# Retention attention and a snake-activated layer on one core: a new order and new engines for all steps, a wait ahead of batch 2's loads, and two banks for the last two sums

## The chip, the core and the metric

The kernel runs on one core of a Trainium2 chip. The metric is the device time of one execution in microseconds. An engine here is one of TensorE (PE in the profile; PEld are its weight loads), VectorE (DVE), ScalarE (ACT), GpSimd (POOL) and SyncE (SP), which only issues transfers.

## What is computed

```python
# q, k, v: (8 batches, 8 heads, 576 positions, 64); gamma[h] = 1 - 2**(-5-h)
scores = q @ k.T / 8
ret    = scores * where(i >= j, gamma[h] ** (i - j), 0)
x      = (ret @ v), heads side by side        # (4608 tokens, 512)
h      = x @ w_in                             # (4608, 2048)
s      = sin(alpha * h)
g      = h + s * s / (alpha + 1e-9)
out    = g @ w_out                            # (4608, 512)
```

## The kernel before, in words

The 4608 tokens are cut into nine blocks of 512: blocks 0 to 7 are positions 0 to 511 of batches 0 to 7, and block 8 gathers the last 64 positions of all eight batches. The decay gamma**(i-j) is folded into q and k when they are cast to fp16, and the attention goes over in chunks of 128 positions with a running state between chunks.

One text, `STEPS`, holds every step of the program in the order in which it is issued. A step is a name, its numbers, and an engine after a colon where there is a choice (V is VectorE, A ScalarE, G GpSimd, P TensorE). Each engine takes its own steps in that order, and waits with semaphores for what they need. A word such as `raw.2.k.1=14` gives a buffer or a PSUM bank its place, so the text also sets when a buffer or a bank is used again. The loop at the end of the function (lines 934 to 954) reads the text; there a word `<NAME` adds a wait for an earlier step.

The steps that the change and the prediction speak of are these, with n the block and u one of the 16 units of 128 columns of `w_in`:

- `LD.b.k.p` (line 432) loads half p of k, q or v of batch b, 512 KB, on SP's queue. `WI.g` and `WO.g` (lines 402, 405) load the quarters of `w_in` and `w_out` on GpSimd's queue and cast them to fp16.
- `CA` (line 455; for v line 332) casts and scales what was loaded. `XP` (line 487) turns k and q with a transposing transfer on SP's queue; batches 0 and 1 are turned on TensorE instead (`TU`, line 473, copied out by `TK`).
- `SC` (line 558) makes scores, `MK` (line 571, VectorE) masks them, `VA` and `VB` (line 589) multiply them with v, `SA` (line 625) adds the state's share, `KP` copies the result out. `OU` (line 506) makes the chunks' state; `EV`, `TS`, `MA`, `MB`, `NS` and `ST` (lines 332 to 545) carry it on.
- `PR.n.u` (line 776) makes one unit of `x @ w_in` in a bank with four products of 512 columns (or two halves of 256). `SI` (line 784, ScalarE) takes the sine, `SQ` squares it (line 794 on ScalarE, 795 on VectorE or GpSimd), `PD` (line 799, VectorE) makes g and so sets the bank free.
- `G2.0.c` (line 815) makes block 0's output. Blocks 1 to 8 use a scheme of seven products for a two by two block matrix (`PP.n.p`, line 882, four groups j each), with sums of parts of g made beforehand by `SM` (line 863) and of `w_out` by `TT` (line 851).
- `CP` copies a product's bank out, `AD` (line 900) adds a bank to it, and `OQ` (lines 906 and 907) writes a quarter of the block to memory with two transfers. For the very last quarter `AD.8.12` and `OQ.8.12` are cut into two halves of 256 columns; the second transfer of each half goes out from ScalarE's queue, the rest from SP's.
- `KB` (line 419) are products with zeros that fill TensorE's waits at the start.

For block 8 the order within product 3 is by halves of the columns: `PP.8.3.0` and `PP.8.3.1` make columns 0 to 255, `PP.8.3.2` and `PP.8.3.3` columns 256 to 511, all in bank Z.

Of the kernel before, what the change touches and what calls it, by code (L numbers as in the profile page):

```python
# [960 lines left out]
```

## Time and profile before

| | |
|---|---|
| median of 3 runs | 302.37 us (302.0 to 302.52) |
| the profiled execution | 303.11 us, span 301.2 us |
| TensorE busy | 288.2 us (96%) |
| VectorE busy | 248.0 us (82%) |
| GpSimd busy | 190.9 us (63%) |
| ScalarE busy | 189.0 us (63%) |
| transfers | 49.88 MB, mean 166 GB/s |

The span is the time from the first to the last instruction; the profiled execution's own time is 1.91 us longer. Busy time is an average over stages that differ: in the first 60 us the weights and the first batches arrive, and the rest is products nearly without a break. TensorE's granted clock stands at 9 or more tenths in all 40 slices. Instructions of one line that follow each other are put together in the timeline, with "x8" for their number, and the time in brackets is how long the engine sat idle before the first of them, and for whom.

### The profile page before, as it was taken

Reading aid. Unit: us, or ns where it says so; the run is one execution under the profiler, and the core shown is the slowest. Engines: PE = TensorE matmul, PEld = TensorE weight load, DVE = VectorE, ACT = ScalarE, POOL = GpSimd, SP = SyncE. Lnnn points to the kernel's source line nnn. Section 1 sums busy time; section 2 is a strip of 40 time slices with the busy share of each in tenths; the row PEclk is TensorE's granted clock in tenths of the full one; section 3 lists DMA queues with packets and bytes.
Section 4 is the critical chain, followed back from the end, with each engine's and each line's share of the span. In section 5 each row is a group of like instructions: output and inputs, shape, how many; then the busy total and the mean of one; then the engine's idle time right before and its main releaser. Section 6 shows DMA issues by size and latency. Waiting matters only on the chain.

```text
span 301.2 us, 8721 instructions
## 1 busy us (share of the span) xinstructions
PE 288.2 (96%) x3625; PEld 185.6 (62%) x3625; DVE 248.0 (82%) x362; ACT 189.0 (63%) x302; POOL 190.9 (63%) x171
## 2 busy tenths in 40 slices
PE   7999999898999999999999999999999999999994
PEld 4665445453666656666675667666666576456883
DVE  2577899988998899998699999899887957579941
ACT  1645952769765895976737765783655366877420
POOL 6747863479858746957698529865755524894320
PEclk9999999999999999999999999999999999999999
DMA  7999999999979699669889773346457072004154
GB/s 226 316 253 232 216 221 316 326 199 257 214 194 249 171 228 180 166 161 152 196 182 195 177 168 98 88 93 143 106 131 134 0 191 55 2 2 104 37 125 119
DMA packets 119510, 49.88 MB, mean 166 GB/s; under 512 B 69792, under 2 KB 118960, under 8 KB 119472
## 3 DMA queue, kind: packets, MB, share of 16 engines
q1 hardware_dynamic: 114880, 44.97, 63.7%
q0 software_dynamic: 4224, 4.19, 8.2%
q8 instruction: 28, 0.46, 0.7%
q10 hardware_dynamic: 368, 0.18, 0.2%
q14 instruction: 10, 0.08, 0.1%
HBM read 36.74 MB, written 9.44 MB: 153 GB/s over the span
## 4 chain that ended last, share of the span: by engine, by line
PE 47%; DVE 5%; ACT 2%; issue 1%; DVEq 0%; ACTq 0%
PE banks L882 23%; PE banks L776 21%; DVE g L799 2%; ACT s L784 1%; ACT s L794 1%; PE banks L558 1%; PE banks L589 1%; DVE r L863 1%; PE banks L506 0%; DVE h L571 0%; DVE h L332 0%; DVE h L455 0%; DVE h L900 0%; DVE h L531 0%; PE banks L625 0%
## 5 line engine op out<-in xcount | busy, mean ns | idle before, releaser
L776 PE MATMUL banks<-r,w_in 128*128 128x512 f16 (+1 forms) x608 | 139.0, 368 | 1.9 <-DVE g L799 1.3
L784 ACT ACTIVATE s<-banks,alpha 128x512 f16<-128x512 f32 x144 | 95.4, 688 | 41.8 <-PE banks L776 39.0
L799 DVE SCALAR_TENSOR_TENSOR g<-s,inva,banks 128x512 f16<-128x512 f16 x144 | 102.4, 741 | 18.8 <-ACT s L794 13.5
L776 PEld LDWEIGHTS <-w_in 128*128 128x128 f16 x608 | 57.4, 98 | 54.7 <-issue 4.1
L882 PEld LDWEIGHTS <-g 128*128 128x128 f16 x640 | 61.4, 98 | 17.1 <-POOL g L863 0.4
L795 POOL TENSOR_TENSOR s<-s 128x512 f16<-128x512 f16 x36 | 38.0, 1060 | 40.0 <-ACT s L784 32.4
L882 PE MATMUL banks<-w_out,g 128*128 128x256 f16 x384 | 50.2, 273 | 0.3 <-DVE g L799 0.3
L332 ACT COPY h<-banks 128x512 f32<-128x512 f32 (+2 forms) x37 | 23.8, 643 | 36.6 <-PE banks L882 25.6
L794 ACT ACTIVATE s<-s 128x512 f16<-128x512 f16 x73 | 44.6, 629 | 2.0 <-PE banks L589 0.7
L455 POOL TENSOR_TENSOR h<-r,cn 128x1024 f16<-128x1024 f32 (+1 forms) x23 | 36.7, 1600 | 12.7 <-DMA r<-in_q_dram 11.8
L863 POOL TENSOR_TENSOR r<-g 128x1024 f16<-128x1024 f16 x15 | 31.9, 2131 | 11.9 <-DVE g L863 7.3
L571 DVE TENSOR_TENSOR h<-banks,mask 128x1024 f16<-128x1024 f32 (+1 forms) x32 | 35.4, 1116 | 4.0 <-PE banks L558 3.9
L882 PE MATMUL banks<-r,g 128*128 128x256 f16 x256 | 34.7, 273 | 0.0
L882 PEld LDWEIGHTS <-r 128*128 128x128 f16 x256 | 25.0, 98 | 6.3
L332 ACT CAST r<-banks 128x1024 f16<-128x1024 f32 (+1 forms) x18 | 16.1, 892 | 14.1 <-PE banks L589 8.0
L900 DVE TENSOR_TENSOR h<-banks,h 128x512 f32<-128x512 f32 (+1 forms) x25 | 16.5, 665 | 8.3 <-PE banks L882 5.6
L795 DVE TENSOR_TENSOR s<-s 128x512 f16<-128x512 f16 x35 | 19.8, 571 | 3.1 <-ACT s L784 3.0
L455 DVE TENSOR_TENSOR h<-r,cn 128x1024 f16<-128x1024 f32 (+1 forms) x17 | 18.4, 1088 | 4.8 <-DMA r<-in_k_dram 4.0
L863 POOL TENSOR_TENSOR g<-g,r 128x1024 f16<-128x1024 f16 x6 | 14.2, 2370 | 7.4 <-DVE r L863 7.4
L534 POOL TENSOR_TENSOR r<-h,r 128x256 f32<-128x256 f32 x12 | 9.4, 784 | 12.5 <-DVE h L531 10.1
L545 POOL TENSOR_TENSOR h<-r,cn 128x256 f16<-128x256 f32 x19 | 14.2, 751 | 3.7 <-DVE r L534 2.1
L882 PE MATMUL banks<-r 128*128 128x256 f16 x128 | 16.3, 273 | 0.0
(67 smaller groups left out, 274.5 us busy)
## 6 DMA issues: line engine op xcount, KB each, us to landing
out_dram<-h SPq DMA_DIRECT2D x70, 128.0 KB, 2.4
r<-in_q_dram SPq DMA_DIRECT2D x16, 512.0 KB, 5.5
r<-in_k_dram SPq DMA_DIRECT2D x10, 512.0 KB, 6.0
r<-in_v_dram SPq DMA_DIRECT2D x10, 512.0 KB, 11.2
r<-in_k_dram SPq DMA_DIRECT2D x24, 128.0 KB, 4.0
r<-in_v_dram SPq DMA_DIRECT2D x24, 128.0 KB, 4.2
w_in<-in_moe_w_in_dram POOLq DMA_DIRECT2D x4, 512.0 KB, 10.0
w_out<-in_moe_w_out_dram POOLq DMA_DIRECT2D x4, 512.0 KB, 13.9
```

The lines of the kernel that those rows point to most:

```text
L332: return eng.copy(d_, s_) if eng is nc.scalar else eng.tensor_copy(d_, s_)
L455: return eng.tensor_tensor(dst[:, a0:a1].rearrange("p a r t d -> p t (a r) d"), t_.rearrange("p (t a) x -> p t a x", t=2)[:, :, a0:a1].rea ...
L545: return eng.tensor_tensor(state_of(b, c), sum_of(b, c), decays(), MULT)
L571: return nc.vector.tensor_tensor(ret(b, p, y).rearrange("p t (z x) -> p (t z) x", z=2)[:, :, 0:n], bank(f"sc.{b}.{p}.{y}", 2).rearrange("p ...
L776: i = matmul(bank(hps)[:, cols], w_in16[:, a, u * P : (u + 1) * P], x_of(n)[:, a, cols], start=starts(hps), stop=(a == KT - 1), skip_group ...
L784: return nc.scalar.activation(small(f"s.{name}")[:, cols], bank(f"hps.{name}")[:, cols], mybir.ActivationFunctionType.Sin, bias=0.0, scale ...
L794: return nc.scalar.activation(ss_t, s_t, mybir.ActivationFunctionType.Square)
L795: return eng.tensor_tensor(ss_t, s_t, s_t, MULT)
L799: return nc.vector.scalar_tensor_tensor(g_of(n)[:, u, cols], small(f"ss.{name}")[:, cols], inva[:, u : u + 1], bank(f"hps.{name}")[:, cols ...
L863: return eng.tensor_tensor(S[s], a, b, op)
L882: i = matmul(ps[:, 256 * c : 256 * c + 256], left[:, 0, 128 * c : 128 * c + 128], right[:, 0, :], start=starts(f"{BANK_OF[p]}.{n}"), stop= ...
L900: return nc.vector.tensor_tensor(x, bank(f"{b}.{n}")[:, cols], x, ADD)
```

## The change

Four things change. The text `STEPS` is written in another order throughout, and many steps have another engine: 30 go from GpSimd to VectorE, 33 from VectorE to GpSimd, 23 each way between VectorE and ScalarE, 17 from GpSimd to ScalarE and 11 the other way (markers of the kind `RL` counted in). `LD.2.k.1`, the first load of batch 2, gets a wait for `WO.1`, and the nine loads after it come in a new order. For block 8, products 5 and 3 write their columns 0 to 255 to bank Z and 256 to 511 to bank Y. And the sum `AD.8.22` is cut into halves as `AD.8.12` was.

```diff
-TS.1.0:A; LD.2.q.0 raw.2.q.0=0; SI.0.12 s.0.12=15; SC.1.0.1 sc.1.0.1=0; PD.0.15; TU.1.k.1.2 tr.1.k.1=2
+TS.1.0:A kvs.1=15; PR.0.13.2 hps.0.13=4; TS.1.1:A; LD.2.k.1 raw.2.k.1=14 <WO.1; MA.1.1:G s32.1.1=27; PD.0.15
...
-PP.8.4.0; PP.8.3.2; CP.8.4:A c21.8=10; PP.8.3.0; OQ.8.21; PP.8.3.1; PP.8.3.3; AD.8.12.0; AD.8.12.1; OQ.8.12.0
-OQ.8.12.1
+PP.8.4.0; OQ.8.22; PP.8.4.2; PP.8.3.1; CP.8.4:A c21.8=10; PP.8.3.0; OQ.8.21; PP.8.3.3; AD.8.12.0; PP.8.3.2; AD.8.12.1
+OQ.8.12.0; OQ.8.12.1
...
     def PP(n, p, j):
-        ps = bank(f"{BANK_OF[p]}.{n}")
+
+        rows = ("Z", "Y") if n == 8 and p in (5, 3) else (BANK_OF[p],) * 2
...
                 i = matmul(
-                    ps[:, 256 * c : 256 * c + 256], left[:, 0, 128 * c : 128 * c + 128], right[:, 0, :],
-                    start=starts(f"{BANK_OF[p]}.{n}"), stop=True, skip_group_check=True,
+                    bank(f"{rows[c]}.{n}")[:, 256 * c : 256 * c + 256],
+                    left[:, 0, 128 * c : 128 * c + 128], right[:, 0, :],
+                    start=starts(f"{rows[c]}.{n}.{p in (5, 3)}"), stop=True, skip_group_check=True,
                 )
...
         cols = slice(0, 512) if h == 2 else slice(256 * h, 256 * h + 256)
+        if h == 1:
+            b = "Y"
```

The first place is SP's queue, where batch 2's loads begin. Before, `LD.1.v.1` and the next eight loads (`r` is the buffer of the loads; DMAHW are the lanes of SP's transfers):

```order
L432 DMA r_67<-in_v_dram 128x8x128 [waits DMAHW6_49]
L432 DMA r_67<-in_k_dram 128x8x128 [waits DMAHW7_49]
L432 DMA r_67<-in_q_dram 128x8x128 [waits DMAHW0_49,DVE_49,Pool_49]
L432 DMA r_67<-in_k_dram 128x8x128 [waits DMAHW1_49,DVE_49]
L432 DMA r_67<-in_v_dram 128x8x128 [waits DMAHW2_49,Activation_49]
L432 DMA r_67<-in_q_dram 128x8x128 [waits DMAHW3_49,DVE_49]
L432 DMA r_67<-in_v_dram 128x8x128 [waits DMAHW4_49,Activation_49]
L432 DMA r_67<-in_q_dram 128x8x128 [waits DMAHW5_49,DVE_49]
```

The same place now (line numbers are one less):

```order
L431 DMA r_67<-in_v_dram 128x8x128 [waits DMAHW6_49]
L431 DMA r_67<-in_k_dram 128x8x128 [waits DMAHW7_49,DMASW5_49]
L431 DMA r_67<-in_q_dram 128x8x128 [waits DMAHW0_49,DVE_49,Pool_49]
L431 DMA r_67<-in_q_dram 128x8x128 [waits DMAHW1_49,DVE_49]
L431 DMA r_67<-in_v_dram 128x8x128 [waits DMAHW2_49,Activation_49]
L431 DMA r_67<-in_k_dram 128x8x128 [waits DMAHW3_49]
L431 DMA r_67<-in_q_dram 128x8x128 [waits DMAHW4_49,DVE_49]
L431 DMA r_67<-in_v_dram 128x8x128 [waits DMAHW5_49]
```

The second row of the new piece is `LD.2.k.1`; DMASW5 is the lane of the second quarter of `w_out` on GpSimd's queue. Batch 2's v.0 moved from the fourth to the seventh of these loads, and batch 2's q.1 and v.1 moved ahead of it.

The second place is VectorE where block 1's first units are finished (the rows of line 799 are `PD.1.13`, `PD.1.6` and so on, line 851 is `TT`, line 795 is `SQ`). Before:

```order
L851 TENSOR_TENSOR r_67<-w_out_65,r_67 128x1024
L455 TENSOR_TENSOR h_68<-r_67,cn 128x2x8x64
L851 TENSOR_TENSOR r_67<-w_out_65,r_67 128x1024
L795 TENSOR_TENSOR s_69<-s_69 128x512
L799 SCALAR_TENSOR_TENSOR g_70<-s_69,inva,banks 128x512 x2
L795 TENSOR_TENSOR s_69<-s_69 128x512
L851 TENSOR_TENSOR r_67<-w_out_65,r_67 128x1024
L799 SCALAR_TENSOR_TENSOR g_70<-s_69,inva,banks 128x512 x3
```

Now:

```order
L850 TENSOR_TENSOR r_67<-w_out_65,r_67 128x1024
L454 TENSOR_TENSOR h_68<-r_67,cn 128x2x8x64
L850 TENSOR_TENSOR r_67<-w_out_65,r_67 128x1024
L798 SCALAR_TENSOR_TENSOR g_70<-s_69,inva,banks 128x512 x2
L794 TENSOR_TENSOR s_69<-s_69 128x512
L850 TENSOR_TENSOR r_67<-w_out_65,r_67 128x1024
L454 TENSOR_TENSOR h_68<-r_67,cn 128x2x8x64
L798 SCALAR_TENSOR_TENSOR g_70<-s_69,inva,banks 128x512 x3
```

The first square, `SQ.1.13`, left VectorE for GpSimd, and a cast of batch 3, `CA.3.q.1`, came to VectorE behind the first two `PD` of block 1.

The third place is the end of VectorE's program, from the sum `AD.8.11` on (line 900 is `AD`, line 332 the copy `CP.7.4`). Before:

```order
L900 TENSOR_TENSOR h_68<-banks,h_68 128x512 x2
L863 TENSOR_TENSOR g_70<-g_70,r_67 128x4x256
L332 COPY h_68<-banks 128x512
L900 TENSOR_TENSOR h_68<-banks,h_68 128x512
L900 TENSOR_TENSOR h_68<-banks,h_68 128x256 x2
```

Now:

```order
L903 TENSOR_TENSOR h_68<-banks,h_68 128x512
L862 TENSOR_TENSOR r_67<-g_70 128x1024
L862 TENSOR_TENSOR g_70<-g_70,r_67 128x4x256
L903 TENSOR_TENSOR h_68<-banks,h_68 128x512
L903 TENSOR_TENSOR h_68<-banks,h_68 128x256 x4
```

The copy went to ScalarE, and the last sums are four halves instead of one whole and two halves.

More of the change, by code (lines that the diff above doesn't have):

```diff
@@ new lines @@
+PR.0.12.2 hps.0.12=6; CA.1.v.0.2:V v16.1.0=22; SQ.0.6:A ss.0.6=4; PR.0.15.1; PD.0.3; SI.0.7 s.0.7=5
+PR.0.14.2 hps.0.14=2; SQ.0.5:V ss.0.5=2; SI.0.12 s.0.12=3; SQ.0.7:V ss.0.7=6; PR.0.10.2 hps.0.10=4; PD.0.7
+SI.0.14 s.0.14=1; SQ.0.9:A ss.0.9=7; PD.0.5; G2.0.3.0 op.0.3=7; SQ.0.14:G ss.0.14=8; SI.0.10 s.0.10=10; PD.0.6
+TU.1.k.0.2 tr.1.k.0=0; SQ.0.10:A ss.0.10=11; PD.0.14; G2.0.1.0 op.0.1=5; SI.0.15 s.0.15=9; PD.0.9
+CA.1.k.1.2:G k16.1.1=23; TK.1.k.0.2:A kT.1.0=24; PD.0.10; OU.1.0 kv.1.0.0=1 kv.1.0.1=2; SQ.0.15:V ss.0.15=12
@@ new lines @@
+CA.2.q.1.2:V q16.2.1=14; PR.1.6.2 hps.1.6=7; LD.3.q.0 raw.3.q.0=11; PR.1.13.1; TT.2.1:V; SI.1.6 s.1.6=14
+PR.1.9.2 hps.1.9=3; CA.2.k.0.2:V k16.2.0=6; SI.1.13 s.1.13=2; PR.1.4.1; FI.0.1:A osb.0.1=7; LD.3.k.0 raw.3.k.0=9
+SQ.1.13:G ss.1.13=6; G2.0.2.3 op.0.2=2; TT.4.1:V T4=12; SQ.1.6:A ss.1.6=5; SI.1.5 s.1.5=1; PR.1.7.2 hps.1.7=5
+CA.2.k.1.0:G; CA.2.v.1.2:A v16.2.1=15; LD.4.k.0 raw.4.k.0=10; PD.1.13 gT.1=1; G2.0.0.2; PD.1.6
+CA.2.v.0.2:A v16.2.0=12; PR.1.3.2 hps.1.3=4; SQ.1.5:V ss.1.5=10; SI.1.7 s.1.7=4; TT.4.0:V; G2.0.2.1
@@ new lines @@
+XP.2.q.1 qT.2.1=23; PR.1.0.0 hps.1.0=3; SI.1.1 s.1.1=1; MB.2.2:G; SC.2.0.1 sc.2.0.1=6; SI.1.10 s.1.10=2; PD.1.8
+PR.1.11.2 hps.1.11=4; FI.0.2:A osb.0.2=22; CA.3.q.0.2:G q16.3.0=21; MK.2.0.1 ret.2.0.1=2; PR.1.2.2 hps.1.2=1
+SI.1.11 s.1.11=14; SI.1.2 s.1.2=4; SC.2.0.0 sc.2.0.0=6; LD.3.v.1 raw.3.v.1=0; PR.1.0.1; ST.2.1:G s16.2=4
+MK.2.0.0 ret.2.0.0=26; SQ.1.2:A ss.1.2=10; XP.3.q.1 qT.3.1=25; ST.2.0:G; SQ.1.10:A ss.1.10=6; CA.3.k.0.1:G
+SI.1.0 s.1.0=7; VA.2.0 o.2.0=6; PD.1.10; SQ.1.11:A ss.1.11=5; RL.2.0:P; SA.2.0; VB.2.0; TT.3.0:V
@@ new lines @@
+PP.4.4.3; PD.5.5; PP.4.3.2; SQ.5.8:A ss.5.8=6; XP.7.k.1 kT.7.1=16; ST.6.2:G; PR.5.9.2 hps.5.9=2; CP.4.4:A c21.4=26
+PD.5.8; RL.6.1:G; MA.6.3:G s32.6.3=19; SQ.5.10:A ss.5.10=11; PP.4.3.1; SM.5.3.1:G; SI.5.9 s.5.9=12
+PR.5.14.2 hps.5.14=1; AD.4.12; SQ.5.9:A ss.5.9=4; PD.5.10; SA.6.1; VA.6.0 o.6.0=6; VB.6.1; PD.5.9
+OU.7.2 kv.7.0=0 kv.7.1=3; RL.6.0:G; MB.6.3:G; KP.6.1.2:A x.6=11; CA.7.q.1.2:V q16.7.1=3; VB.6.0; SA.6.0
+PP.5.1.1 X.5=2; SI.5.14 s.5.14=14; PR.5.12.2 hps.5.12=4; KP.6.0.2:A; SM.5.1.0:V; XP.7.q.1 qT.7.1=15
@@ L230 @@
+CP.8.2:A p2.8=11; PP.7.3.2; AD.8.11; PP.7.3.1; PP.7.4.0; SM.8.2.1:V; PP.8.6.0; SM.8.4.0:V; SM.8.4.1:G; PP.8.6.3
+PP.8.6.1; AD.7.12; PP.8.6.2; OQ.7.12; PP.8.5.3 Z.8=3; CP.8.6:A u2.8=6; PP.8.5.1; CP.7.4:A c21.7=18; PP.8.7.0; OQ.7.21
+PP.8.7.1; PP.8.7.3; PP.8.7.2; PP.8.5.0; OQ.8.11; CP.8.7:A u3.8=22; PP.8.5.2; PP.8.4.1; AD.8.22.0; PP.8.4.3; AD.8.22.1
+PP.8.4.0; OQ.8.22; PP.8.4.2; PP.8.3.1; CP.8.4:A c21.8=10; PP.8.3.0; OQ.8.21; PP.8.3.3; AD.8.12.0; PP.8.3.2; AD.8.12.1
+OQ.8.12.0; OQ.8.12.1
 """
```

382 lines of the change are left out of this document (179 added, 203 removed).

## The prediction

> **What bounds the kernel now.** I read the page's head first, then a table of stretches, then who waits for whom on TensorE in the stretches that leave it idle, then the timeline there and at the end.
>
> ```profile
> span 301.2 us, 8721 instructions
> PE 288.2 (96%) x3625; PEld 185.6 (62%) x3625; DVE 248.0 (82%) x362; ACT 189.0 (63%) x302; POOL 190.9 (63%) x171
> ...
> PE 47%; DVE 5%; ACT 2%; issue 1%; DVEq 0%; ACTq 0%
> ```
>
> TensorE is busy 288.2 us of 301.2, and the chain that ended last runs mostly over it. The change adds and removes no product of the reference, so it can only win back idle time: 301.2 - 288.2 = 13.0 us in all. The table of stretches says where that lies (us from A to B, length, then TensorE's busy time and instructions, then its weight loads, VectorE, ScalarE, GpSimd, the granted clock, the transfers' share and GB/s):
>
> ```profile
> 0.00:21.00 21.00, 18.25 (x328) 12.23 (x329) 10.76 (x18) 9.23 (x13) 13.16 (x25) 1.00 1.03 259
> 21.00:28.20 7.20, 7.03 (x55) 4.42 (x51) 5.27 (x9) 3.86 (x7) 5.59 (x6) 1.00 1.19 261
> 28.20:63.50 35.30, 32.79 (x372) 17.02 (x372) 32.49 (x50) 21.95 (x35) 18.94 (x20) 1.00 1.16 263
> 63.50:78.00 14.50, 12.36 (x214) 6.50 (x213) 13.02 (x16) 12.92 (x23) 13.19 (x14) 1.00 0.99 230
> 78.00:284.00 206.00, 205.00 (x2556) 134.26 (x2550) 179.90 (x262) 138.73 (x222) 137.89 (x108) 1.00 0.61 135
> 284.00:296.80 12.80, 12.73 (x117) 11.15 (x115) 5.83 (x10) 2.34 (x4) 2.12 (x1) 1.00 0.51 124
> 296.80:301.20 4.40, 0.00 (x0) 0.00 (x0) 0.72 (x2) 0.00 (x0) 0.00 (x0) 1.00 0.48 119
> ```
>
> Idle: 2.75 us before 21, 0.17 to 28.2, 2.51 to 63.5, 2.14 to 78, only 1.00 in the 206 us after that, and 4.40 after the last product. The granted clock is 1.00 throughout, so nothing is to be had there. Between 28.2 and 78 VectorE is busy 32.49 of 35.30 and 13.02 of 14.50 us: it is the engine that TensorE waits for. The waits of TensorE from 21 to 78 agree:
>
> ```profile
> PE banks L589 <- DVE h L571: 1.3, 1, 1.3
> PE banks L776 <- DVE g L799: 1.3, 2, 1.1
> PE banks L558 <- DVE g L799: 0.7, 2, 0.4
> PE banks L558 <- ACT r L332: 0.4, 1, 0.4
> PE banks L506 <- DVE g L799: 0.3, 1, 0.3
> ```
>
> **The start, up to 28.2 us.** The attention of block 0 is issued in a new order there, with other engines for small copies. But the units of `PR` that follow need `w_in`, and the second quarter sets when they go on (weight loads of TensorE):
>
> ```profile
> 28.19 1.84 PEld L776 LDWEIGHTS <-w_in 128*128 128x128 f16 x10 [0.42 <-DMA w_in<-in_moe_w_in_dram]
> ```
>
> `PR.0.4` waits for that landing now, with all work that could be done before it done. Whatever the start gains is idle again before 28.2 us, so I cost all of it at nothing. If the start lost more than these 0.42 us the cover would be gone, and each further us would count in full. One thing gets worse: `TU.1.q.0` stood ahead of this wait and now stands behind `PR.0.4`, so its eight products (an estimate of 0.45 us: the sixteen narrower ones of `SC.2.0.0` take 0.42 below) move from idle time into the busy stretch.
>
> **28.2 to 63.5 us: up to 2.51 us.** The longest wait is for `PD.1.6` on VectorE, which sets a bank free, and VectorE was late because of one square:
>
> ```profile
> 56.70 2.12 DVE L795 TENSOR_TENSOR s<-s 128x512 f16<-128x512 f16 x1 [0.32 <-ACT s L784]
> 58.93 1.41 DVE L799 SCALAR_TENSOR_TENSOR g<-s,inva,banks 128x512 f16<-128x512 f16 x2
> 60.25 0.42 DVE L795 TENSOR_TENSOR s<-s 128x512 f16<-128x512 f16 x1
> ...
> 56.64 3.08 POOL L455 TENSOR_TENSOR h<-r,cn 128x1024 f16<-128x1024 f32 x2 [7.88 <-DMA r<-in_q_dram]
> ...
> 60.39 1.46 PE L776 MATMUL banks<-r,w_in 128*128 128x512 f16 x8 [1.13 <-DVE g L799]
> ```
>
> `SQ.1.13` took 2.12 us, where the same square took 0.42 at 60.25. It began 0.06 us after the first of two casts on GpSimd (3.08 for both), and ended while these were still running. The change sends this square to GpSimd, where one takes 1.06 us, and the cast to VectorE, behind `PD.1.6`:
>
> ```profile
> 26.97 1.06 POOL L795 TENSOR_TENSOR s<-s 128x512 f16<-128x512 f16 x1
> 32.77 1.04 POOL L332 CAST h<-r 128x1024 f16<-128x1024 f32 x1
> 54.55 1.22 DVE L455 TENSOR_TENSOR h<-r,cn 128x1024 f16<-128x1024 f32 x1
> ```
>
> In VectorE's queue ahead of `PD.1.13` the change takes out this 2.12 and about five small operations like the 0.42 one (`TS.1.1`, `TK.1.k.1.1`, `SQ.0.13`, `MA.1.2`, `ST.1.2`): 4.2 us. It puts in `SQ.0.15`, `SQ.0.12` and `ST.0.3` (0.42 each) and the cast `CA.1.v.0`, which VectorE hasn't done in that form; between the 0.42 of a small operation and the 1.22 us of its scaled cast I take 1.0, near the 1.04 of GpSimd's cast: 2.3 us. VectorE is ahead by about 1.9 us. The square's longer way (1.06, then 0.70 for `PD`, 1.41 / 2, and ahead of both a sine for which I put the same 0.7 as an estimate: 2.5 us) lies beside `PR.1.9`, half of `PR.1.4`, `PR.1.7` and two `G2`, which now stand before the next user of its bank; at 0.22 us for a product of 512 columns (below) that is 18 x 0.22 = 3.9 us, enough. So the 1.13 us go. Of the other 2.51 - 1.13 = 1.38 us, those for `OU.1.0` and `TU.1.k.1` lose their cause in part, because `PR.0.13` was moved up behind `OU.1.0`; but `PR.1.13` now follows soon behind `KP.1.0`, and `PR.1.6` behind `FI.0.3`. I take two thirds, 0.9. Less the 0.45 of `TU.1.q.0`: 1.13 + 0.9 - 0.45 = **1.6 us gained**; ends 0 and 2.5.
>
> **The wait on `WO.1`.** On SP's queue all loads and transposes of batches 2 to 4 stand behind it.
>
> ```profile
> 25.41 1.55 POOL L405 DMA_DIRECT2D w_out<-in_moe_w_out_dram  x2
> ...
> DMA to landing us min/median/max: 12.8/13.9/16.6
> ...
> 24.58 7.07 SPq L432 DMA_DIRECT2D r<-in_k_dram  x1
> 31.78 7.06 SPq L432 DMA_DIRECT2D r<-in_q_dram  x1
> 52.07 2.87 SPq L432 DMA_DIRECT2D r<-in_k_dram  x2
> ```
>
> `WO.1` is issued at 25.41 and lands 13.9 us later by the median of the four, at 39.3. Batch 2's first loads sit 7 us each in SP's queue before that, since the transfers are full (1.16 in the table), so holding `LD.2.k.1` to 39.3 mostly replaces one queue by another. GpSimd now makes `WO.0` behind a cast that waits for a load, and `WO.1` behind `SQ.0.0`, some 2.5 us later; the quarters of `w_in` are still under way then, so I let the landing stand, with 13.9 us from about 28, 41.9, as the late end. From there seven loads at 1.4 us (2.87 / 2) bring v.0 of batch 2 at about 50 to 53, and its user `OU.2` comes near 62. I cost the wait at nothing; the cover is about 8 us.
>
> **63.5 to 78 us: up to 2.14 us.**
>
> ```profile
> 70.78 0.42 PE L558 MATMUL banks<-h 64*64 64x128 f16 x16
> 72.53 0.95 PE L589 MATMUL banks<-h 64*64 64x128 f16 x32 [1.33 <-DVE h L571]
> ...
> 75.68 0.21 PE L558 MATMUL banks<-h 64*64 64x128 f16 x1 [0.25 <-DVE g L799]
> 76.33 0.41 PE L558 MATMUL banks<-h 64*64 64x128 f16 x15 [0.44 <-DVE g L799]
> ...
> 256.65 8.74 PE banks L776 x40
> ```
>
> `VA.2.0` stands straight behind the scores `SC.2.0.0` and waits 1.33 us for their mask. The change puts the half unit `PR.1.0.1` between: two products' worth, 2 x 0.22 (8.74 / 40) = 0.44 us. `SC.2.1.0` waits 0.25 + 0.44 us for two `PD`; it now has `PR.1.14` ahead of it, 0.87 us, so these 0.69 go. Sum 1.13. But both halves' scores now stand together, so `MK.2.1.0` and `MK.2.1.1` follow each other before `VA.2.1`, some 0.1 us short: **1.0 us gained**, ends 0 and 2.1.
>
> **78 to 296.8 us.** There are 1.00 us idle in the long stretch, so little can be won and anything can be lost: every place where a bank is used again was moved. The covers that I counted in both orders are alike, and two became shorter behind block 7's scores (`PR.6.9` and `PR.6.12`, by 0.2 and 0.4 us). I take **0.3 us lost**, with ends of 1.0 gained (all the idle time) and 2.0 lost (two new waits, each like the longest two that TensorE has now, 1.13 and 1.33 us, less a little).
>
> **The end.**
>
> ```profile
> 294.82 1.91 PE L882 MATMUL banks<-w_out,g 128*128 128x256 f16 x16
> 296.77 0.76 DVE L900 TENSOR_TENSOR h<-banks,h 128x256 f32<-128x256 f32 x2 [2.73 <-PE banks L882]
> 296.27 0.60 SPq L907 DMA_DIRECT2D out_dram<-h  x1
> 297.22 1.13 SPq L906 DMA_DIRECT2D out_dram<-h  x2
> 297.27 1.35 ACTq L907 DMA_DIRECT2D out_dram<-h  x2
> ```
>
> The last 16 products are `PP.8.3`. VectorE's two half sums both start after the last of them, from 296.77 on (0.76 for both), although the first half's columns were complete earlier; then each queue issues two transfers in a row, and ScalarE's second is out at 297.27 + 1.35 = 298.62. With two banks the first half's eight products come first and the sum of bank Z can run beside the other eight, ready at about 296.3. ScalarE then issues its first transfer at once; SP is held by `OQ.8.21` until 296.87 and issues to 297.45. The second sum runs 296.77 to 297.19, its transfers are out at 298.05 on SP (297.45 + 0.57 + a gap) and 297.9 on ScalarE. **0.6 us gained** (298.62 - 298.05); ends 0 (the sum still waits) and 0.7. The halved `AD.8.22` adds about 0.1 us on VectorE, which idles there, beside the four groups of `PP.8.4`.
>
> **The sum.** 1.6 + 1.0 - 0.3 + 0.6 = 2.9 us less. The profiled execution had 303.11 us (span 301.2 and 1.91 around it): 300.2. The median of the runs is 302.37, 0.74 lower, and a median is what is predicted: 302.37 - 2.9 = 299.5 us.
>
> **The rivals.**
>
> *The arrivals take over.* The 1.16 and 0.99 of the transfers' share up to 78 us speak for it: where VectorE is no longer late, block 1's v or the last quarters of `w_out` are, and batch 2's come as they did. Against it: in the list of TensorE's waits there VectorE ends 3.6 of the 4.0 us. Then only the end is won: 302.37 - 0.6 = 301.8 us. Chance 0.12.
>
> *VectorE is held by GpSimd where TensorE waits for it (slower).* The row of 2.12 us beside one of 0.42 shows that a square can lose 1.7 us on VectorE while GpSimd works. The change brings 30 steps from GpSimd to VectorE; between 28.2 and 63.5 us `SQ.0.15`, `SQ.0.12` and `ST.0.3` are such, and `CA.3.q.1` there takes the place of a cast. Three at 1.7 are 5.1 us, against 2.9 gained: 302.37 - 2.9 + 5.1 = 304.6. It turns slower from the second one on (3.4 > 2.9). Against it: VectorE gives 33 steps away, and most squares there ran at their short time (VectorE's line 795 has 35 in 19.8 us). Chance 0.13.
>
> ```profile
> L795 DVE TENSOR_TENSOR s<-s 128x512 f16<-128x512 f16 x35 | 19.8, 571 | 3.1 <-ACT s L784 3.0
> ```
>
> The Trainium skill, SBUF — State Buffer, section "Who interferes with whom", has it as a rule: a VectorE operation with two inputs in SBUF and a GpSimd one that reads SBUF exclude each other for a whole instruction, whichever starts first. The 2.12 us fit it. By this rule alone each of the three would stand behind whatever GpSimd runs then, and the time would be the 304.6 of this rival; the mean of 0.57 us for a square says that most don't meet one.
>
> *The wait doesn't matter and neither does the order.* The early gains are given back by new waits after 78 us (the 2.0 end) and the end's sum still waits: 302.37 - 2.6 + 2.0 = 301.8 at best, 302.4 if the end loses what it may. Chance 0.05.
>
> **How the numbers follow.** The forecast has 0.70. Faster or slower by over 0.2% is 0.6 us either way, about what a measurement of this kernel can tell. Forecast: faster. The rival of the arrivals lies on that border: 0.05 faster, 0.07 same. The last: same 0.05. The held VectorE: 0.13 slower. So 0.75, 0.12, 0.13. The low end takes about the terms' gains at their better ends in part: 302.37 - (2.2 + 1.6 + 0.5 + 0.7) = 297.4. The high end reaches over the border rivals to 302.4, and what is left out is the slower rival.
>
> **What would show it.** Right: no wait of 1 us for VectorE's line of `PD` near 60 us; the state of batch 2 (`OU.2`) starting near 62 instead of 63.5; `VA.2.0` waiting under 1 us; VectorE's first of the last two sums starting before the last product ends, and the last transfer issued about 1.3 us after that product instead of 1.9. Wrong: squares of 1 to 2 us on VectorE between 28 and 63 us; SP's first load of batch 2 issued after 45 us with TensorE waiting for a load of batch 2; or more than 3 us idle between 78 and 284 us.

## The result, and the profile after

The changed kernel takes 305.0 us (median of 12 executions, 302.61 to 308.07) where before takes 302.43 in the same series. The ratio is 1.0074, 95% interval 1.0048 to 1.0100: slower by 2.2 us, where 2.9 us less was forecast. The ratios, here and below, leave out executions over 1.5% above the fastest of their kernel (308.07 and 307.58 of the twelve here), while the medians count all. The profiled execution of it took 304.19 us. The new order is also less even: it spreads over 5.5 us, and ten of the twelve executions of before lay between 302.00 and 303.21.

Line numbers of the kernel after are one less than before up to the sums; `AD` is line 903, `OQ` lines 909 and 910. First the head of its page.

```profile
span 302.4 us, 8716 instructions
PE 287.8 (95%) x3625; PEld 186.3 (62%) x3625; DVE 247.2 (82%) x360; ACT 189.6 (63%) x307; POOL 180.3 (60%) x169
...
PE 72%; DVE 12%; DMA 4%; issue 3%; ACT 3%; SPq 3%; POOL 2%; DVEq 0%; POOLq 0%
```

TensorE works as long as before (287.8 against 288.2 us) in a span that is 1.2 us longer. The chain that ended last runs 12% over VectorE and 4% over transfers; the 5% for VectorE before belong to a chain that the page follows over 55% of the span only. The stretches of the kernel after, with the same columns as in the prediction; the last two are set to where its last product ends:

```profile
0.00:21.00 21.00, 18.50 (x329) 13.07 (x330) 12.74 (x23) 8.05 (x12) 12.39 (x23) 1.00 1.04 260
21.00:28.20 7.20, 6.50 (x43) 3.91 (x42) 4.00 (x8) 4.67 (x8) 4.65 (x5) 1.00 1.19 259
28.20:63.50 35.30, 34.35 (x448) 18.71 (x449) 32.10 (x51) 23.09 (x40) 17.83 (x21) 1.00 1.13 257
63.50:78.00 14.50, 12.83 (x162) 7.04 (x160) 13.58 (x16) 13.27 (x24) 13.02 (x14) 1.00 1.06 228
78.00:284.00 206.00, 201.60 (x2522) 131.34 (x2522) 177.62 (x254) 136.00 (x219) 127.73 (x109) 1.00 0.64 135
284.00:298.00 14.00, 14.00 (x129) 12.25 (x126) 6.75 (x12) 4.55 (x8) 4.66 (x2) 1.00 0.53 127
298.00:302.40 4.40, 0.02 (x1) 0.00 (x0) 0.42 (x1) 0.00 (x0) 0.00 (x0) 0.77 0.45 119
```

Length less TensorE's busy time is its idle time. Against before:

| stretch | idle before | idle after | difference | forecast |
|---|---|---|---|---|
| to 28.2 us | 2.92 | 3.20 | +0.28 | 0 |
| 28.2 to 63.5 | 2.51 | 0.95 | -1.56 | -1.6 |
| 63.5 to 78 | 2.14 | 1.67 | -0.47 | -1.0 |
| 78 to the last product | 1.07 | 4.40 | +3.33 | +0.3 |
| behind it | 4.40 | 4.38 | -0.02 | -0.6 |

These are +1.56 us idle; with 0.36 us less busy that is the 1.2 us of the spans. The two executions that were profiled are nearer to each other than the kernels are: 304.19 us is one of the faster ones of the new order (305.0 is its median), and before's 303.11 lies above ten of the twelve of before in this series. So the table shows the places of the loss, and less than its whole size. The early gain came, and the long stretch after 78 us, where before had 1.00 us idle in 206, took back twice as much. TensorE's waits there, in the kernel after:

```profile
PE banks L624 <- issue: 1.7, 1, 1.7
PE banks L588 <- DVE g L798: 1.3, 1, 1.3
PE banks L557 <- DVE h L570: 0.7, 1, 0.7
PE banks L882 <- DVE h L903: 0.4, 1, 0.4
PE banks L588 <- DVE h L570: 0.4, 1, 0.4
```

Three of them are large, and each has another cause. The first, in the timeline, is `SA.5.1` (line 624, 16 small products):

```profile
170.53 0.41 PE L624 MATMUL banks<-h 64*64 64x128 f16 x15
...
172.66 0.24 PE L624 MATMUL banks<-h 64*64 64x128 f16 x1 [1.72 <-issue]
```

TensorE stops after 15 of 16 products that read the same buffers and write the same two banks, and nothing that the profile follows ends the wait ("issue"). The second is `VA.7.1` (line 588), near 231 us:

```profile
229.63 2.13 POOL L862 TENSOR_TENSOR r<-g 128x1024 f16<-128x1024 f16 x1
229.69 2.35 DVE L794 TENSOR_TENSOR s<-s 128x512 f16<-128x512 f16 x1
...
232.07 1.41 DVE L798 SCALAR_TENSOR_TENSOR g<-s,inva,banks 128x512 f16<-128x512 f16 x2
...
232.87 0.36 PE L588 MATMUL banks<-h 64*64 64x128 f16 x15 [1.33 <-DVE g L798]
```

`SQ.6.14` takes 2.35 us on VectorE: it starts 0.06 us after `SM.6.2.0` on GpSimd and ends 0.28 us after it, then `PD.6.14` sets the bank free that `VA.7.1` needs. This is the picture of `SQ.1.13` before, at another place. The third is `SC.4.1.1` (line 557), which waits for the mask `MK.4.1.0` to empty its banks, and that mask waits for a transfer:

```profile
121.59 0.62 SPq L909 DMA_DIRECT2D out_dram<-h  x1
...
122.26 0.62 SPq L910 DMA_DIRECT2D out_dram<-h  x1
...
124.79 1.23 DVE L570 TENSOR_TENSOR h<-banks,mask 128x1024 f16<-128x1024 f32 x1 [0.90 <-DMA out_dram<-h]
...
126.07 0.42 PE L557 MATMUL banks<-h 64*64 64x128 f16 x16 [0.67 <-DVE h L570]
```

The mask's result goes to place 17 of the middle-sized buffers, which held block 1's last quarter until `OQ.1.12` had read it; that output was issued at 121.59 and 122.26, though its sum `AD.1.12` had ended at 99.66.

The end, from `AD.8.12.0` on:

```profile
297.19 0.42 DVE L903 TENSOR_TENSOR h<-banks,h 128x256 f32<-128x256 f32 x1 [1.90 <-PE banks L882]
297.56 0.61 SPq L910 DMA_DIRECT2D out_dram<-h  x1
297.69 1.41 ACTq L910 DMA_DIRECT2D out_dram<-h  x2
298.06 0.42 DVE L903 TENSOR_TENSOR h<-banks,h 128x256 f32<-128x256 f32 x1 [0.45 <-PE banks L882]
298.27 1.19 SPq L909 DMA_DIRECT2D out_dram<-h  x2
```

The first half's sum does run beside the last products, and ScalarE's first transfer goes out at 297.69, ahead of their end (298.02). But SP is held by `OQ.8.21` until 298.17 and issues both its transfers after that, to 299.46, 1.44 us behind the last product where ScalarE's last was 1.89 behind it before (298.62 less 296.73).

### The profile page after: what moved, and what is told of

Same layout as the page of the kernel before. It is cut to its first block, busy times and chain, and to the rows that moved or that the text cites. A ratio compares the mean times of both kernels' runs of the same rounds, so it can differ in the third digit from the quotient of the medians.

```text
span 302.4 us, 8716 instructions
## 1 busy us (share of the span) xinstructions
PE 287.8 (95%) x3625; PEld 186.3 (62%) x3625; DVE 247.2 (82%) x360; ACT 189.6 (63%) x307; POOL 180.3 (60%) x169
## 4 chain that ended last, share of the span: by engine, by line
PE 72%; DVE 12%; DMA 4%; issue 3%; ACT 3%; SPq 3%; POOL 2%; DVEq 0%; POOLq 0%
PE banks L775 32%; PE banks L882 28%; DVE g L798 4%; DVE h L570 3%; DMA w_in<-in_moe_w_in_dram 3%; PE banks L814 3%; PE banks L557 2%; PE banks L418 2%; PE banks L588 2%; SPq L427 2%; ACT s L783 1%; PE banks L505 1%; DVE s L794 1%; PE banks L624 1%; DVE h L331 1%
## 5 line engine op out<-in xcount | busy, mean ns | idle before, releaser
L775 PE MATMUL banks<-r,w_in 128*128 128x512 f16 (+1 forms) x608 | 137.6, 368 | 1.5 <-DMA w_in<-in_moe_w_in_dram 0.7
L794 POOL TENSOR_TENSOR s<-s 128x512 f16<-128x512 f16 x29 | 31.4, 1089 | 40.4 <-ACT s L783 34.9
L793 ACT ACTIVATE s<-s 128x512 f16<-128x512 f16 x81 | 50.0, 630 | 1.8 <-PE banks L588 0.3
L454 POOL TENSOR_TENSOR h<-r,cn 128x1024 f16<-128x1024 f32 (+1 forms) x25 | 38.9, 1561 | 5.9 <-DMA r<-in_q_dram 5.0
L862 POOL TENSOR_TENSOR r<-g 128x1024 f16<-128x1024 f16 x11 | 23.6, 2154 | 30.9 <-DVE g L862 17.3
L331 ACT CAST r<-banks 128x1024 f16<-128x1024 f32 (+1 forms) x15 | 13.4, 899 | 14.7 <-PE banks L624 6.8
L862 POOL TENSOR_TENSOR g<-g,r 128x1024 f16<-128x1024 f16 x7 | 16.7, 2381 | 5.1 <-DVE r L862 3.4
L794 DVE TENSOR_TENSOR s<-s 128x512 f16<-128x512 f16 x34 | 17.4, 515 | 0.5 <-ACT s L783 0.3
L882 PE MATMUL banks<-w_out,r 128*128 128x256 f16 x128 | 16.8, 273 | 0.0
L862 DVE TENSOR_TENSOR r<-g 128x1024 f16<-128x1024 f16 x21 | 16.6, 794 | 0.2
```

The source lines that it names most:

```text
L331: return eng.copy(d_, s_) if eng is nc.scalar else eng.tensor_copy(d_, s_)
L454: return eng.tensor_tensor(dst[:, a0:a1].rearrange("p a r t d -> p t (a r) d"), t_.rearrange("p (t a) x -> p t a x", t=2)[:, :, a0:a1].rea ...
L775: i = matmul(bank(hps)[:, cols], w_in16[:, a, u * P : (u + 1) * P], x_of(n)[:, a, cols], start=starts(hps), stop=(a == KT - 1), skip_group ...
L793: return nc.scalar.activation(ss_t, s_t, mybir.ActivationFunctionType.Square)
L794: return eng.tensor_tensor(ss_t, s_t, s_t, MULT)
L862: return eng.tensor_tensor(S[s], a, b, op)
```

## The experiments

Fourteen kernels ran, in series of two to four that share a chip and their own executions of before (median 302.78 to 303.06 us). All ratios are to before in the same series. The intervals are 0.2 to 0.4% wide to each side, so terms under about 1 us are read from profiles, not from times.

**Where the loss is: the two halves of the program.** At 78 us both orders have done exactly the same steps, so they can be joined there. `front_new` has the new order up to `LE.2.q` and before's behind it; `rest_new` the reverse.

```diff
 ...; CA.3.v.1.0:A; RL.2.1:G; SM.1.1.0:G; PP.1.2.1      (before, up to here)
-XP.3.k.1; PD.1.14; VB.2.1; SA.2.1; ...
+LE.2.q; VB.2.1; SA.2.1; PD.1.14; ...                    (rest_new: the new order from here)
```

> The changed order up to 78 us (from the start to the loads LE.2.q), the order, engines, places and end of before behind it. Theory (the early gain is real, and the later order loses it again through waits of its own): the products VA.2.0 start near 70.6 us as in the changed kernel, 1.9 us earlier than before, and the time is about 1.9 us under before, 300.5. Rival (the gain is only borrowed, VectorE gives it back within the next 60 us whatever the order): VA.2.0 is early as well, but the time is that of before, 302.4.

Measured: 302.43 us, ratio 0.9978 (0.9952 to 1.0005), 0.7 us under before; by the interval, anything from 1.5 under to 0.2 over. The 1.9 us expected lie outside it.

> The order of before up to 78 us (VB.2.1), everything of the changed kernel behind it, with its two banks at the end. Theory: the later order waits whenever it comes there, 3.2 us more than before's, so about 305.6. Rival (it waits only because TensorE comes 1.9 us early): 302.4 to 303.5.

Measured: 307.21 us, ratio 1.0087 (1.0052 to 1.0123), 2.6 us over before. With front_new that adds up to +1.9, near the whole change's 2.2: the loss lies in the later order, and it is there when TensorE comes at before's time (`VA.2.1` starts at 79.32 us here, at 79.85 before). The rival allowed 1.1 us over before at most, and 2.6 (1.6 to 3.7 by the interval) is more. Front_new's 0.7 us fall short of the 1.9 expected, and its rival's nothing lies within the interval: in before's order, too, part of the early gain doesn't reach the end. Its profiled execution was the slowest of its twelve (306.17, with `VA.2.0` at 72.55 us and not at 70.6), so where that part goes stays open. TensorE's waits from 120 to 180 us in rest_new show two of the three waits. They are longer, but in one of its slower executions (309.52), so their places count here and not their sizes:

```profile
PE banks L557 <- DVE h L570: 2.8, 1, 2.8
PE banks L588 <- issue: 2.7, 1, 2.7
```

**Do the waits come back?** `new_again` is the changed kernel once more.

> The changed kernel as it is, for a second profile. Theory: 305.0, and the waits of SA.5.1 near 170 us (1.7 us for nothing that the profile shows) and of VA.7.1 near 231 us (1.3 us for PD.6.14) come back at the same places. Rival (accidents of one execution): other places, or none.

Measured: 305.81 us, ratio 1.0076 (1.0048 to 1.0105). Its waits from 120 to 240 us:

```profile
PE banks L624 <- issue: 1.4, 1, 1.4
PE banks L588 <- DVE g L798: 1.3, 1, 1.3
PE banks L557 <- DVE h L570: 0.8, 1, 0.8
```

Same places, same order. The waits belong to the order, not to one execution; only their size varies.

**TensorE's own instructions.** In the trace, 4545 of TensorE's instructions (weight loads, products and the few that only handle semaphores) come before the stop at `SA.5.1`, in the kernel after and in new_again; and in rest_new 4545 come before its stop, which is at the first product of `VB.5.1`. 4545 is 17 x 256 + 193, and the trace holds 28 transfers of 16 KB on an instruction queue (on the page "q8 instruction: 28, 0.46", for TensorE's 7250 weight loads and products), one for some 256 of them. In the kernel after one of these starts at 170.41 us and takes 0.95; TensorE goes on at 172.66. `shifted` moves the rest of the program by 172 places, with more but smaller products with zeros at the start.

```diff
-            matmul(banks[:, b, 0:m], zero[:, 0:P], zero[:, 0:m], start=True, stop=True)
+            w = 16 if m <= 128 else P
+            matmul(banks[0:w, b, 0:m], zero[:, 0:w], zero[:, 0:m], start=True, stop=True)
...
-KB.14.384.3 ... KB.14.256.2
+KB.70.64.3 ... KB.44.128.2
```

> The changed kernel, but the first two groups of products with zeros are 70 and 44 small ones instead of 14 and 14, so that all later instructions of TensorE stand 172 places further on in its program; their time is about the same. Theory (TensorE waits for the next 256 of its own instructions, which come in one transfer): the wait at SA.5.1 (1.9 us) and the 0.6 us ahead of PR.2.7.2 are gone, and no other place has so dense a run of products at a border; about 2 us under the changed kernel. Rival (a wait for data or for a bank): both waits stay where they are, and the time too.

Measured: 306.8 us, ratio 1.0130 (1.0102 to 1.0157). Between 160 and 180 us the wait of 1.7 is gone, what is left is 0.2. But there is a new one near 20 us, in block 0's `OU` (line 506 in this kernel):

```profile
20.12 0.22 PE L506 MATMUL banks<-h 64*64 64x64 f16 x3 [0.90 <-issue]
```

705 instructions come before it, which is 2 x 256 + 193. So the wait follows the border of 256 and not the step: the theory holds for `SA.5.1`, but the 2 us that it forecast did not come, for the border fell on another dense run of small products, at the start. The 0.9 us there are part of the 1.6 us by which this kernel comes late to `VA.2.0` (72.18 against 70.62); what else made it slower than new_again was not followed up. Ahead of `PR.2.7.2`, the other place named, the traces show no wait; the one just behind it, 0.4 us at `PP.1.6.0` for a sum on VectorE, is there in both kernels, 172 places further on in shifted: that one isn't a border.

What makes the transfer late at 170 us was tried by moving transfers on SP's queue, `XE.1.q` in one kernel, `LD.7.q.0` and `LD.7.q.1` in the other:

```diff
 xe_later:  -... PR.4.11.2; XE.1.q; SQ.4.10:A ...     +... RL.5.1:A; XP.6.q.1; XE.1.q; MA.6.2:G ...
 q7_later:  -... LD.7.q.0 ... LD.7.q.1 ...            +... RL.5.1:A; XP.6.q.1; LD.7.q.0; LD.7.q.1; MA.6.2:G ...
```

> The changed kernel with one transposing transfer, XE.1.q, moved on SP's queue from ahead of LD.7.k.1 to behind XP.6.q.1, some 6 us later. Theory (TensorE waits at SA.5.1 for its next 256 instructions, whose transfer is held up by this transpose): the 16 KB transfer starts by 168 us instead of 169.7 to 170.4, the wait of 1.6 to 1.9 us goes. Rival (it is held up by the 1 MB of the loads LD.7.q.0 and LD.7.q.1 issued just before): the wait stays.

> The changed kernel with the loads LD.7.q.0 and LD.7.q.1 moved behind XP.6.q.1 on SP's queue; XE.1.q stays ahead of LD.7.k.1. If the loads hold up the transfer of instructions, the wait at SA.5.1 goes here and stays where only XE.1.q is moved; if the transpose does, it stays here, or comes 1.3 us earlier with it. If neither (a wait for data at SA.5.1), it stays in both.

Measured: xe_later 307.4 us, ratio 1.0106 (1.0069 to 1.0143); q7_later 304.81, ratio 1.0046 (1.0013 to 1.0079). The waits from 120 to 240 us of xe_later:

```profile
PE banks L557 <- DVE h L570: 3.3, 1, 3.3
PE banks L588 <- DVE g L798: 1.3, 1, 1.3
PE banks L624 <- issue: 0.8, 1, 0.8
```

and of q7_later:

```profile
PE banks L557 <- DVE h L570: 2.2, 1, 2.2
PE banks L588 <- DVE g L798: 1.3, 1, 1.3
```

Of these two kernels, the wait for instructions goes only in the one where the two loads go. From the start of `VA.5.0`, the 16 KB transfer begins 2.7 to 5.0 us later in the six profiles with both loads just ahead of it (after 4.3, new_again 3.4, rest_new 5.0, sq_oq 2.7, no_wait 2.9, xe_later 3.2), and 1.2 to 1.8 us later in the seven where they are elsewhere and nothing else stops TensorE (q7_later 1.7, three_edits 1.2, before 1.3, and front_new, tail_new, before_sq13, before_two). In four_edits and five_edits the loads are elsewhere too, but VectorE stops TensorE for 0.9 and 1.1 us on the way, and it is 2.5 and 3.3. How long TensorE waits follows from how late the transfer is: nothing at 2.7, then 0.4 (2.9), 0.8 (3.2), 1.4 (3.4), 1.7 (4.3) and 2.7 us (5.0). So the rival of xe_later is right: a megabyte of loads holds the transfer up, the transpose doesn't; and with the loads there the wait can still be nothing, as in sq_oq. The Trainium skill, Runtime: NRT & Kernel Launch, section "Instruction fetch mechanics", says that a program streams in blocks of 256 instructions, and that crossing a border is "mostly hidden"; blocks and borders agree with this trace, and at 27 of the 28 transfers in the kernel after no such wait of 0.4 us or more shows; at the other it cost 1.7 us.

**The other two waits.** Two edits at once, since they lie 100 us apart and each can be read from the profile.

```diff
-SQ.6.14:V
+SQ.6.14:A
...
-LD.6.v.1; ... PP.2.7.3; OQ.1.12; SI.3.4 ...
+LD.6.v.1; OQ.1.12; ... PP.2.7.3; SI.3.4 ...
```

> The changed kernel with two edits: the square SQ.6.14 goes from VectorE to ScalarE, and the output transfer OQ.1.12 is issued three places earlier on SP's queue, ahead of LD.5.v.1. Theory (two of the later order's waits have these causes: a square held for 2.35 us beside GpSimd's SM.6.2.0, and a mask that waits until OQ.1.12 has left its buffer): the 1.3 us at VA.7.1 and the 0.7 to 0.9 us at SC.4.1.1 go, about 2.0 us under the changed kernel, 303.5 where that has 305.5. Rival (other waits stand right behind): both go, but the time falls by less than 0.7 us.

Measured: 303.52 us, ratio 1.0016 (0.9985 to 1.0047); against new_again's 1.0076 that is 0.6%, 1.8 us (0.5 to 3.1 by the two intervals). Both waits are gone. Its waits from 78 to 298 us are:

```profile
PE banks L557 <- DMA h<-h: 1.0, 1, 1.0
PE banks L588 <- DVE h L570: 0.4, 1, 0.4
PE banks L882 <- DVE h L903: 0.3, 1, 0.3
```

The theory fits, though the time alone would not rule out the rival's 0.7 us. A new wait of 1.0 us for a transpose shows at `SC.5.0.1` in this execution.

**All three, and further.** `three_edits` adds q7_later's move. `four_edits` puts `LD.7.k.0` behind `XP.6.k.0` besides. `five_edits` has, beside the three, `OQ.1.11` behind `LD.5.v.1` and `LD.6.k.1` behind `XP.6.k.0`.

```diff
 four_edits:  -... LD.7.k.0; PD.3.10 ...     +... XP.6.k.0; LD.7.k.0; VB.4.1 ...
 five_edits:  -... LD.6.k.1; PD.3.4 ...      +... XP.6.k.0; LD.6.k.1; VB.4.1 ...
              -... PP.2.5.0; OQ.1.11 ...     +... LD.5.v.1; OQ.1.11 ...
```

> The changed kernel with SQ.6.14 on ScalarE, OQ.1.12 earlier, and LD.7.q.0 and LD.7.q.1 behind XP.6.q.1. Theory (the three waits add up: SC.4.1.1 0.7 to 3.4 us, SA.5.1 0 to 2.9, VA.7.1 1.3): about 1 us under the kernel with the first two edits, near 302.5, and no wait over 0.5 us at the three places. Rival (other waits take their place): the same as with two edits, 303.5.

Measured: 301.67 us, ratio 0.9978 (0.9951 to 1.0005). None of the three waits is left from 78 us to the end:

```profile
PE banks L882 <- DVE h L903: 0.4, 1, 0.4
PE banks L588 <- DVE h L570: 0.4, 1, 0.4
PE banks L775 <- ACT h L331: 0.3, 1, 0.3
PE banks L588 <- issue: 0.2, 1, 0.2
```

From 1.0076 to 0.9978, three edits out of 1489 steps are worth 1.0% (0.6 to 1.4 by the two intervals), about 3 us: as much as the whole later order had lost. It leaves the kernel at front_new's ratio.

> The same with one edit more: the load LD.7.k.0 stands behind the transposes XP.5.q.0, XP.5.k.0, XP.5.k.1 and XP.6.k.0 on SP's queue instead of ahead of them. With two edits SC.5.0.1 near 140 us waited 1.0 us for a transpose to land. Theory: that wait goes, and with it 0.5 us in the median; together under before, about 302. Rival (SP's queue is not what makes the transposes late, their casts are): the wait stays.

Measured: 302.7 us, ratio 1.0006 (0.9982 to 1.0030), not under three_edits but 0.8 us over it. `SC.5.0.1` doesn't wait here, but it doesn't in three_edits' profile either, so this says nothing of the edit. In this execution ScalarE's copy `CP.2.4` waits, and TensorE behind it. ScalarE's waits from 128 to 137 us:

```profile
ACT h L331 <- DMA h<-h: 2.3, 1, 2.3
```

The copy's buffer was the input of the transpose `XP.5.q.1`, which had to be over first.

> The changed kernel with the three edits (SQ.6.14 on ScalarE, OQ.1.12 earlier, LD.7.q.0 and LD.7.q.1 later) and two more on SP's queue: OQ.1.11 goes out behind LD.5.v.1 already, and LD.6.k.1 stands behind XP.6.k.0, so that XP.5.q.1 has nothing but its own cast ahead of it. Theory (the copy CP.2.4 waits for that transpose, whose input it overwrites): the wait of 0.6 to 2.3 us at PR.3.11.2 near 132 us goes, and the time is 0.3 to 0.8 us under the three edits. Rival (the wait moves to the next buffer or transpose): the same as with three edits.

Measured: 304.25 us, ratio 1.0034 (1.0002 to 1.0067), worse than with three. `CP.2.4` doesn't wait in its profile, and the next copy of its kind does, VectorE's from 160 to 168 us:

```profile
DVE h L331 <- DMA h<-h: 1.9, 1, 1.9
```

This is `CP.3.4`, written into the buffer that the transpose `XP.6.q.0` reads; it waited 1.6 us in four_edits and not at all in three_edits. So the theory is wrong and the rival's picture fits: what waits there moves from buffer to buffer when SP's queue is reordered. With one profile of each kernel, and `CP.2.4` at 0, 0.6 and 2.3 us in sq_oq, three_edits and four_edits, the edits and the spread can't be told apart. That SP has hardly a free moment there fits (it issues without a gap over 0.5 us from 91 to 173 us in the kernel after, and had gaps of 2.20, 1.18 and 1.23 us from 91 to 138 before), but five_edits has a gap of 2.76 us from 124.26 on; that this is the whole of the remaining spread was not shown.

**The wait on `WO.1`.** sq_oq without it:

```diff
-LD.2.k.1 raw.2.k.1=14 <WO.1
+LD.2.k.1 raw.2.k.1=14
```

> The changed kernel with the first two edits (SQ.6.14 on ScalarE, OQ.1.12 earlier) and without the wait of LD.2.k.1 for WO.1. My forecast's step (the wait costs nothing and brings nothing): OU.2.2 starts at 62.0 as with it, and the time is that of the two edits within 0.5 us. Rival (the wait protects the quarters of the weights): the quarters of w_out land later, the products G2 of block 0 or the units before 40 us wait longer, and it is 1 us slower. Rival (it holds batch 2 up): OU.2.2 starts earlier and it is faster.

Measured: 303.17 us, ratio 1.0016 (0.9991 to 1.0042), the same ratio as with the wait. SP's queue with the wait (kernel after):

```profile
39.13 0.37 SPq L431 DMA_DIRECT2D r<-in_k_dram  x1
...
44.70 2.41 SPq L431 DMA_DIRECT2D r<-in_v_dram  x1
```

and without it:

```profile
25.27 7.06 SPq L431 DMA_DIRECT2D r<-in_k_dram  x1
...
43.95 2.92 SPq L431 DMA_DIRECT2D r<-in_v_dram  x1
```

The first load stands in the queue for 7 us instead of waiting ahead of it, and by the fourth load both queues are within 0.8 us. `OU.2.2` starts at 61.90 us without, at 61.99 with the wait. TensorE comes to it no later and no earlier, so both rivals are out.

**The early terms alone.** `before_sq13` is before with only the square and the cast exchanged; `before_two` adds the half unit.

```diff
 before_sq13:  -SQ.1.13:V ... CA.3.q.1.2:G; G2.0.0.3 ...    +SQ.1.13:G ... SQ.1.5:V; CA.3.q.1.2:V ...
 before_two:   -SC.2.0.1; SI.1.11; PR.1.0.1 ...             +SC.2.0.0; SI.1.1; PR.1.0.1 ...
```

> Before with the square SQ.1.13 on GpSimd and the cast CA.3.q.1 on VectorE behind SQ.1.5, nothing else. My forecast's step: the wait of 1.13 us ahead of PR.1.3 near 60 us goes, OU.2.2 starts about 1.1 us earlier, at 62.4; if nothing gives it back, 0.9 to 1.1 us under before. Rival (the engines and transfers behind it set the pace up to 78 us): OU.2.2 is earlier, VA.2.0 at 72.5 is not, and the time is that of before.

Measured: 301.47 us, ratio 0.9960 (0.9940 to 0.9981), 1.2 us under before, the fastest of all that ran. VectorE and TensorE near 60 us in it:

```profile
56.70 1.04 POOL L795 TENSOR_TENSOR s<-s 128x512 f16<-128x512 f16 x1 [8.00 <-ACT s L784]
...
57.78 1.41 DVE L799 SCALAR_TENSOR_TENSOR g<-s,inva,banks 128x512 f16<-128x512 f16 x2 [1.46 <-POOL s L795]
...
59.24 1.46 PE L776 MATMUL banks<-r,w_in 128*128 128x512 f16 x8
```

The square takes 1.04 us on GpSimd, the two `PD` follow, and `PR.1.3` starts at 59.24 instead of 60.39 with no wait ahead of it. The gain lasts to the end (`VA.2.0` 0.98 us earlier, the last product 1.87 us in these two executions), so the rival is out.

> Before with SQ.1.13 on GpSimd and CA.3.q.1 on VectorE, as in the first such kernel, and the half unit PR.1.0.1 moved from behind SC.2.0.1 to behind SC.2.0.0, ahead of VA.2.0. My forecast's step: the wait of VA.2.0 for its mask falls from 1.33 to 0.9 us and VA.2.0 starts 0.4 us earlier than in that kernel, at 71.1; 0.4 us under it. Rival (the time is set by what follows): VA.2.0 is earlier and the time is not.

Measured: 302.42 us, ratio 0.9972 (0.9947 to 0.9998). From the start of `PR.1.3`, `VA.2.0` comes after 12.00 us instead of 12.31, but `VA.2.1` after 19.00 instead of 19.05: `SC.2.1.0` now waits 0.4 us for a `PD` instead. The rival is right, the move alone gains nothing.

**The end.** `tail_new` is before with the new steps from `PP.8.4` on and the two banks. In before's order one group of product 5 goes ahead of product 2's last ones, so that here they add up in one bank, and block 8's output differs; the instructions and their waits are those of the change.

```diff
-PP.8.4.1; AD.8.22; PP.8.4.3; PP.8.4.2 ... PP.8.3.1; PP.8.3.3; AD.8.12.0; AD.8.12.1
+PP.8.4.1; AD.8.22.0; PP.8.4.3; AD.8.22.1 ... PP.8.3.3; AD.8.12.0; PP.8.3.2; AD.8.12.1
```

> Before with the changed end alone: from PP.8.4 on the new order, the last sums in two banks, AD.8.22 in halves. By my forecast 0.6 us under before; by the changed kernel's profile 0.1 to 0.5, since SP's queue holds the first of the last transfers. Rival: no difference within 0.2.

Measured: 302.85 us, ratio 0.9988 (0.9961 to 1.0015), which doesn't tell the theories apart. In the profiles the span ends 4.39 us after the last product here, 4.38 in the kernel after, 4.45 before: 0.1 us. (Before's row in the table of stretches starts 0.07 us behind its last product.)

## Why the prediction was wrong

**The step that failed** is the term for 78 to 296.8 us: 0.3 us lost, with 2.0 as its end. It measured 3.3 us idle, and 2.6 us in rest_new's time. I had counted the products between uses of a bank, found them alike in both orders, and made that the whole risk. None of the three large waits is a bank used too soon by itself. One is a buffer in SBUF that a queued output still has to leave (0.7 to 3.3 us), one is a VectorE square behind GpSimd (1.3), one is TensorE's own program behind two loads (0 to 2.7). For all three the place where they bite is set by what the new order puts next to what, on SP's queue and on GpSimd, and these I had not walked beyond 78 us. The sign that the prediction named for this came true: TensorE was idle for 4.40 us between 78 and 284 us, more than the 3 it gave.

**28.2 to 63.5 us** was right in size and cause: 1.6 forecast, 1.56 in the profile, `OU.2.2` at 62.01 where about 62 was forecast, and the square alone, moved in before, is worth 1.2 us. In the time of a whole kernel less of it shows: front_new, which has all the early terms, gained 0.7 us. Why is not shown.

**63.5 to 78 us** gave 0.47 instead of 1.0. Two of TensorE's waits from 21 to 78 us in the kernel after show why:

```profile
PE banks L588 <- DVE h L570: 0.8, 1, 0.8
...
PE banks L775 <- DVE g L798: 0.6, 2, 0.3
```

`VA.2.0` waits 0.79 us where 0.9 was worked out, so the half unit did its part. But of the 0.69 us for two `PD`, which were to go, 0.34 moved to `PR.1.14`, and `VA.2.1` waits 0.36 us for its mask where 0.1 was put.

**The start** was right at nothing, within 0.3 us, and **the wait on `WO.1`** at nothing: it landed by 39.13 us where 39.3 was worked out, and no_wait has the same ratio.

**The end** was forecast at 0.6 and gave 0.1. The sum ran beside the products as said, and the last issue comes 1.44 us behind the last product instead of 1.89. What I had overlooked is SP's queue: its two transfers start after `OQ.8.21`, its packets end 2.68 us behind the last product, as they did before (2.72), and only ScalarE's, at 3.02 before, came earlier (2.28).

**The rivals.** The one that came true in its sign is the held VectorE, with a chance of 0.13, and its mechanism is one of the three; but I had put it between 28 and 63 us, where nothing of the kind happened, and priced it as the whole. The rule quoted from the Trainium skill, SBUF — State Buffer, section "Who interferes with whom", that the two engines exclude each other for a whole instruction, fits all the long squares: in the sixteen profiles fifty squares on VectorE took over 0.7 us, and each ends 0.28 to 0.29 us after a GpSimd instruction that began before it (`SQ.6.14` 232.04 against 231.76; `SQ.1.13` before 58.82 against 58.54). The rival of gains given back late had the right shape, and too small a price for it (2.0).

## What to carry to other kernels

When a hand-made order is changed throughout, the terms that were aimed at are the easy part; walk every queue that the new order feeds, and look for a buffer that is written soon after the transfer that reads it, for short VectorE operations on SBUF beside long GpSimd ones, and for dense runs of small products where loads are queued. Make the small edit alone first: one square moved to another engine gave 1.2 us in the old order, while the new order with it lost 2.2. Cut the program where both orders have done the same steps and join the halves; two runs then say in which half the loss is.

## What the runs showed of the hardware

- TensorE's program came in 28 transfers of 16 KB, and all six waits of 0.4 us or more that the profiles call "issue" behind 15 us stand at the same place of a block of 256 (193 instructions into it): behind 4545 in the kernel after, new_again, rest_new, xe_later and no_wait (0.4 to 2.7 us), behind 705 in shifted (0.9). In all six TensorE goes on 1.3 to 1.6 us after the transfer's packet ends. What decided at 4545 is how soon the transfer starts (1.2 to 5.0 us from the same step); that the density of the instructions matters too is argued from the two places, both in runs of small products, and was not tested.
- The same wait for a transferred buffer was 0.7, 0.8, 1.1, 2.2, 2.8 and 3.3 us in six profiles with the same steps around it (`SC.4.1.1`; 2.8 is from one of the slower executions). It was a spread of times, not one number. It may be one part of why the new order is so uneven; without it sq_oq still spread from 301.27 to 307.19.
- A granted clock of 0.997 on average, in the changed kernel's profile, comes from the stretch behind the last product (0.77 in the row of 298.00 to 302.40); up to there it was 1.00.
